# One list schedule for the whole program: the Strassen products of the first feed-forward product laid, four tiles at a time, between the matmuls of the second

## The chip, the core and the metric

The kernel runs on one core of a Trainium2 chip. The core has five engines with a queue of instructions each, worked off in order: TensorE (PE, matmuls into PSUM), VectorE (DVE), ScalarE (ACT), GpSimd (POOL) and SyncE (SP, which only issues transfers here). An engine waits on semaphores for the results of others. PSUM, where matmuls put their sums, has eight banks of 128 partitions by 512 fp32 values. The metric is the device time of one execution in microseconds (us), lower is better.

## The reference

Attention over keys and values pooled by eight, and then a feed-forward net with a PReLU. There are 8 batches of 576 tokens, 8 heads of 64, a model width of 512 and an inner width of 2048.

```python
k_p = k.reshape(B, H, Sp, pool, D).mean(axis=3)
v_p = v.reshape(B, H, Sp, pool, D).mean(axis=3)
scores = scale * np.matmul(q, k_p.transpose(0, 1, 3, 2))
scores = scores - np.max(scores, axis=-1, keepdims=True)
attn = np.exp(scores)
attn = attn / (np.sum(attn, axis=-1, keepdims=True) + 1e-09)
return np.matmul(attn, v_p).astype(np.float32)
...
x = np.ascontiguousarray(attn_out.transpose(0, 2, 1, 3)).reshape(B * S, H * D)
...
h = x @ w_in
g = np.maximum(h, 0.0) + alpha * np.minimum(h, 0.0)
return (g @ w_out).astype(np.float32)
```

## The kernel before

**Work and tiles.** The 4608 tokens are cut into nine chunks `c` of 512. Each fp32 operand is split into a high and a low fp16 part, and a product is three fp16 matmuls (low by high, high by low, high by high). `attention` makes a chunk's `x`; it is a chain over all engines with few and short PE instructions: maxima spread by a matmul (`pm`, L216), scores (`s`, L638), softmax, a transposing transfer to `aT`, and the mix with v (`x`, L648). The chain of chunk `c + 1` runs beside the feed-forward work of chunk `c`.

**The first feed-forward product** makes `h` in 16 tiles `f` of 128 inner columns. Chunks 0 and 1 take it plainly (`ffn1_products`, L814 to L816: 12 matmuls of 512 columns for a tile, 192 for a chunk). From chunk 2 on it is done after Strassen (`_Strassen`): four tiles are a block `b`, and a block is seven products of 12 matmuls of 256 columns (`product`, L936, psum tile `m`) where the plain way has eight; a chunk has 4 blocks, 28 products, 336 matmuls. DVE adds each finished product into two SBUF tiles `c` (`after`, L948, seven adds in a block; ACT copies the first one, L944), and `finish` scales (ACT, L960), applies the PReLU (DVE, L961) and splits into the fp16 pair `g` (ACT L962, POOL L963). The sums of the first weight that Strassen needs are made once, on POOL (`v`, L886), DVE (`u`, L889, four instructions, and `o`, L891) and ACT (L890), and kept in DRAM (`combine_w1`, eight steps `q`, during chunk 1); `weights` loads them back as `wt`, two for a block.

**The second product** (`ffn2`, L861 to L863) takes one of the chunk's four row tiles `i` at a time and runs over all 16 `f`: 48 matmuls of 512 columns into one bank, then ACT scales (`out_tile`, L851) and SP stores. It starts when the chunk's whole first product is through PE; so a chunk is one stretch of 336 short matmuls that DVE and POOL must follow, and one of 192 long ones that they need not.

**What sets the order.** Chunk 0, the weights' conversion and chunk 1's attention are laid by `start` with `_Plan`, a list scheduler in Python: each operation has an engine, an assumed duration, what it comes after, a rank and a buffer that it takes or gives; at each step the operation that can start first is issued, the lowest rank among near ones. `fill` puts idle matmuls (`idle`, L977) on PE where the plan sees a gap. From chunk 1 on the code is a plain loop, with the attention of the next chunk put in by counts (`behind`), and the compiler's own scheduler orders each engine's queue. PSUM is split into two tiles of two banks for attention and the conversion (`ps_s`) and four banks `ps_h`, which `m`, `h` and the output sums `o` share:

```python
ps_s = ctx.enter_context(tc.tile_pool(name="ps_s", bufs=2, space=PSUM))
ps_h = ctx.enter_context(tc.tile_pool(name="ps_h", bufs=4, space=PSUM))
...
            self.t[b, m] = ps = ps_h.tile([P, 2, HC], F32, tag="h", name="m")
            for p in range(2):
                for j in range(2):
                    w, x = self.lhs(2 * b + p, m, j), self.rhs(m, j)
                    for n, (lw, lx) in enumerate(((1, 0), (0, 1), (0, 0))):
                        nc.tensor.matmul(ps[:, p], w[:, lw], x[:, lx], start=(j == n == 0), stop=(j == 1 and n == 2))
...
    for b, m in [(b, m) for b in range(NB) for m in st.ORDER]:
        st.product(b, m)
        st.after(b, m)
        behind(-(-count // 25))
for i in range(TPC):
    ffn2(c, i)
    if i == 1:
        line.emit(mixes)
```

Of the kernel before, what the change touches and what calls it, by code (L numbers as in the profile page):

```python
# [13 lines left out]
ALU = mybir.AluOpType  # L14
# [46 lines left out]
def _new_b(c):  # L61
# [5 lines left out]
RK = dict(k_pool=2, ps1=5, ps2=8, s_pool=1, w2_dve=16, lo_dve=0, l1=226.38, step=42.02, l2=393.26, mx1=-998.39,  # L67
          mx1s=146.92, mx2=151.73, mx2s=21.09, grp=-5.46, grps=18.67, cv1=-108.04, cv1s=79.11, r2=-1083.65,
          cv2=835.35, cv2s=693.76, low1=871.6, low2=549.58, lo1=1355.61, lo2=54.48, sc=-185.32, pre=-1204.82,
          hi=-825.73, lo=214.7, step2=-280.35, a1=-96.45, al=2295.88, td=1395.43, ld1=71.07, ld2=2796.7,  # L70
          q0=-256.62, v0=75.31, sm0=125.88, sms0=20.85, mix0=-1030.58, q1=660.03, v1=140.65, sm1=189.37,
          sms1=-273.93, mix1=311.26)


ROOM = dict(d=3, W=8, L=4, f=4, e=3, v=3)
STEADY = dict(f=3, e=2, v=4)


class _Plan:
# [12 lines left out]
    def __init__(self, fill, **room):  # L92
        self.fill = fill
        self.ops, self.room, self.port = [], {k: n * [0.0] for k, n in room.items()}, 0.0

    def add(self, engine, us, emit, *after, rank=0.0, take=None, give=None, two=False):
        op = dict(engine=engine, us=us, emit=emit, after=after, rank=rank, n=len(self.ops),
                  take=take, give=(give,) if isinstance(give, str) else give or (), end=None,
                  two=two or engine == "Pool")
        self.ops.append(op)  # L100
        return op

    def start(self, op, free):
        if any(d["end"] is None for d in op["after"]) or (op["take"] and not self.room[op["take"]]):
            return None
        t = [free.get(op["engine"], 0.0)] + [d["end"] for d in op["after"]]
        if op["take"]:
            t.append(min(self.room[op["take"]]))
        if op["two"]:
            t.append(self.port)  # L110
        return max(t)

    def emit(self):
        free, left = {}, list(self.ops)
        while left:
            best = {}
            for op in left:
                t = self.start(op, free)
                if t is not None:
                    best.setdefault(op["engine"], []).append((t, op))  # L120
            picks = []
            for ready in best.values():
                t0 = min(t for t, _ in ready) + self.NEAR[ready[0][1]["engine"]]
                picks.append(min((x for x in ready if x[0] <= t0), key=lambda x: (x[1]["rank"], x[1]["n"])))
            t, op = min(picks, key=lambda x: (x[0], x[1]["n"]))
            if op["engine"] == "PE":
# [3 lines left out]
            free[op["engine"]] = t + op["us"]  # L130
            if op["two"]:
                self.port = t + op["us"]
            op["end"] = t + op["us"] + (self.DMA_HOP if op["engine"] == "SP" else self.HOP)
            if op["take"]:
                self.room[op["take"]].remove(min(self.room[op["take"]]))
            for kind in op["give"]:
                self.room[kind].append(op["end"])
            op["emit"]()
            left.remove(op)
# [3 lines left out]
def pooled_attention_prelu_ffn(ctx: ExitStack, tc: tile.TileContext, qT, kT, vT, kN, vN, w1, w2, alpha, out):  # L143
# [15 lines left out]
    gp = ctx.enter_context(tc.tile_pool(name="gp", bufs=NB))  # L159
    ps_s = ctx.enter_context(tc.tile_pool(name="ps_s", bufs=2, space=PSUM))  # L160
    ps_h = ctx.enter_context(tc.tile_pool(name="ps_h", bufs=4, space=PSUM))
    room = dict(ROOM)
    work = ExitStack()
    fp = work.enter_context(tc.tile_pool(name="fp", bufs=room["f"]))
# [700 lines left out]
    def ffn2(c, i):  # L865
        ps = ps_h.tile([P, DM], F32, tag="h", name="o")
        for f in range(NF):
            ffn2_step(c, i, f, ps)
# [253 lines left out]
```

## Time and profile before

| | us |
|---|---|
| median of 3 runs | 913.65 (913.49 to 917.79) |
| the profiled execution, its own time | 915.54 |
| its span, first to last instruction | 913.8 |
| PE busy | 824.7 |
| DVE busy | 608.3 |
| ACT busy | 459.6 |
| POOL busy | 410.2 |

The span is what the views of the trace divide up; the execution's own time is 1.74 us more. Busy time is a sum over the whole program and hides that DVE is nearly full in some stretches and nearly empty in others. A matmul's own duration is longer than the distance to the next one, since they are pipelined; what a stretch of matmuls costs is read from PE's busy time over the stretch, divided by their number. PEclk is the share of TensorE's full clock (2.4 GHz) that was granted; at 1.2 GHz it is a half.

### The profile page before, as it was taken

What the parts mean: (1) busy time and instruction counts of PE and PEld (TensorE: products, weight loads), DVE (VectorE), ACT (ScalarE), POOL (GpSimd) and SP (SyncE); (2) the same over time, 40 slices, a digit from 0 to 9 for tenths busy, and PEclk for the clock granted to TensorE, in tenths of its full rate; (3) what the DMA queues carried; (4) which work ended last, traced back from release to release, by engine and by line L of the source; (5) the groups of instructions that cost most, each with busy time, mean ns of one, the idle gap of its engine ahead of it and who ended that gap; (6) DMA issues with size and microseconds to landing.
All of it is one profiled execution on the core that took longest, in us unless ns stands there. A gap on an engine that the chain in (4) does not pass through costs nothing.

```text
span 913.8 us, 14931 instructions
## 1 busy us (share of the span) xinstructions
PE 824.7 (90%) x5953; PEld 503.4 (55%) x5953; DVE 608.3 (67%) x938; ACT 459.6 (50%) x760; POOL 410.2 (45%) x384
## 2 busy tenths in 40 slices
PE   6689988967998889979997999789978999899998
PEld 5454443423446744765475646654666468547843
DVE  5889997899537974597449844984499229733710
ACT  6879983635444464436335633563356336632420
POOL 1266577486505480357134823672247205800520
PEclk9979999988999899989999999999989999999999
DMA  9688323732644456427442754374437404902200
GB/s 340 228 239 340 98 65 81 244 123 88 151 141 144 146 150 172 148 89 226 128 154 103 208 128 155 125 218 117 154 129 207 115 24 163 249 28 82 104 14 33
DMA packets 106197, 133.68 MB, mean 146 GB/s; under 512 B 78320, under 2 KB 80944, under 8 KB 106128
## 3 DMA queue, kind: packets, MB, share of 16 engines
q1 hardware_dynamic: 106128, 132.74, 47.2%
q8 instruction: 46, 0.75, 0.3%
q14 instruction: 23, 0.19, 0.1%
HBM read 96.48 MB, written 16.78 MB: 124 GB/s over the span
## 4 chain that ended last, share of the span: by engine, by line
PE 51%; DVE 27%; ACT 7%; DMA 5%; issue 5%; POOL 5%; SPq 0%; DVEq 0%; ACTq 0%; POOLq 0%
PE o L861 12%; PE o L862 11%; PE o L863 11%; PE m L936 11%; DVE c L961 5%; DVE c L948 4%; DVE u L889 3%; POOL g L963 2%; DMA w<-w_dram 2%; DVE q L451 2%; PE x L648 2%; DMA ws<-o 2%; PE idle L977 2%; DVE t L824 1%; DVE o L891 1%
## 5 line engine op out<-in xcount | busy, mean ns | idle before, releaser
L936 PEld LDWEIGHTS <-wt 128*128 128x128 f16 x2352 | 230.5, 99 | 59.3 <-issue 26.9
L862 PE MATMUL o<-w,g 128*128 128x512 f16 x544 | 207.7, 382 | 2.9 <-POOL w L747 2.9
L963 POOL TENSOR_TENSOR g<-c,g 128x512 f16<-128x512 f32 x112 | 139.8, 1272 | 155.9 <-ACT g L962 151.7
L861 PE MATMUL o<-w,g 128*128 128x512 f16 x544 | 206.8, 383 | 1.0 <-DVE c L948 1.0
L863 PE MATMUL o<-w,g 128*128 128x512 f16 x544 | 206.6, 381 | 0.0
L948 DVE TENSOR_TENSOR c<-m,c 128x512 f32<-128x512 f32 x196 | 128.7, 680 | 93.7 <-PE m L936 91.7
L936 PE MATMUL m<-x,wt 128*128 128x256 f16 x1344 | 164.0, 278 | 13.5 <-DVE c L948 11.9
L472 POOL TENSOR_TENSOR vraw<-vraw 72x512 f32<-72x512 f32 (+1 forms) x56 | 59.9, 1090 | 179.6 <-DMA vraw<-vT_dram 145.9
L936 PE MATMUL m<-xt,wt 128*128 128x256 f16 x1008 | 123.4, 277 | 10.4 <-DVE c L948 10.4
L961 DVE SCALAR_TENSOR_TENSOR c<-c,al 128x512 f32<-128x512 f32 x112 | 108.0, 992 | 4.8 <-ACT c L960 4.8
L851 ACT ACTIVATE o<-o,os 128x512 f32<-128x512 f32 x34 | 23.3, 687 | 163.9 <-PE o L863 163.9
L960 ACT ACTIVATE c<-c,rp 128x512 f32<-128x512 f32 x112 | 73.3, 712 | 49.4 <-DVE c L948 49.3
L863 PEld LDWEIGHTS <-g 128*128 128x128 f16 x576 | 56.8, 99 | 72.3 <-issue 5.4
L861 PEld LDWEIGHTS <-g 128*128 128x128 f16 x576 | 56.9, 99 | 70.6 <-issue 3.9
L862 PEld LDWEIGHTS <-g 128*128 128x128 f16 x576 | 56.8, 99 | 66.9 <-issue 2.1
L962 ACT CAST g<-c 128x512 f16<-128x512 f32 x112 | 65.1, 615 | 30.4 <-DVE c L961 29.8
L601 DVE TENSOR_TENSOR xf<-xf 128x256 f32<-128x256 f32 x56 | 23.8, 424 | 84.4 <-ACT xf L596 82.9
L814 PE MATMUL h<-x,w 128*128 128x512 f16 x128 | 51.7, 404 | 11.2 <-ACT t L820 9.9
L546 ACT CAST apad<-e 128x576 f16<-128x576 f32 x72 | 44.7, 668 | 32.5 <-POOL e L541 27.8
L541 POOL TENSOR_TENSOR e<-e,sm 128x576 f32<-128x576 f32 x35 | 44.8, 1281 | 31.9 <-DVE sm L539 10.6
L835 POOL TENSOR_TENSOR g<-t,g 128x512 f16<-128x512 f32 x32 | 42.3, 1330 | 29.0 <-ACT g L832 28.9
L815 PE MATMUL h<-x,w 128*128 128x512 f16 x128 | 51.9, 405 | 2.9 <-DVE x L580 2.9
(152 smaller groups left out, 1092.9 us busy)
## 6 DMA issues: line engine op xcount, KB each, us to landing
wt<-ws SPq DMA_DIRECT2D x56, 896.0 KB
w<-w_dram SPq DMA_DIRECT2D x16, 1024.0 KB
out_dram<-o SPq DMA_DIRECT2D x36, 256.0 KB
qraw<-qT_dram SPq DMA_DIRECT2D x17, 512.0 KB
vraw<-vT_dram SPq DMA_DIRECT2D x28, 288.0 KB
kraw<-kT_dram SPq DMA_DIRECT2D x12, 576.0 KB
ws<-o SPq DMA_DIRECT2D x8, 512.0 KB
ws<-w SPq DMA_DIRECT2D x8, 256.0 KB
```

The lines of the kernel that those rows point to most:

```text
L472: nc.gpsimd.tensor_tensor(out=o, in0=y, in1=z, op=ALU.add)
L814: nc.tensor.matmul(ps, w[:, 1, ks_], x[:, 0], start=(n == 0), stop=False)
L815: nc.tensor.matmul(ps, w[:, 0, ks_], x[:, 1], start=False, stop=False)
L861: nc.tensor.matmul(ps, g[:, 1, ts_], w[:, 0], start=(f == 0), stop=False)
L862: nc.tensor.matmul(ps, g[:, 0, ts_], w[:, 1], start=False, stop=False)
L863: nc.tensor.matmul(ps, g[:, 0, ts_], w[:, 0], start=False, stop=(f == NF - 1))
L936: nc.tensor.matmul(ps[:, p], w[:, lw], x[:, lx], start=(j == n == 0), stop=(j == 1 and n == 2))
L948: nc.vector.tensor_tensor(out=self.part(b, *o), in0=ps, in1=self.part(b, *i), op=ALU.add)
L960: nc.scalar.activation(u, u, AF.Copy, scale=rp[:, f:f + 1])
L961: nc.vector.scalar_tensor_tensor(out=u, in0=u, scalar=al[:, f:f + 1], in1=u, op0=ALU.mult, op1=ALU.max)
L962: nc.scalar.copy(out=g[:, 0, p], in_=u)
L963: nc.gpsimd.tensor_tensor(out=g[:, 1, p], in0=u, in1=g[:, 0, p], op=ALU.subtract)
```

## The change

1. `start` no longer issues its plan: the rest of the program is added to the same `_Plan`, and one list schedule orders all five engines from the first instruction to the last. The numbers in `RK` and the room for buffers are new; the first stage's plan has new ranks.
2. `steady` lays PE's order for chunks 1 to 8: the items of a block of the first product (seven Strassen products, or four plain tiles) and eight pieces of the second product of the block before, in turn. A piece is one row tile `i` with two of the block's four `f`, six matmuls; the four row tiles are summed over the chunk in the four banks of `ps_h`, and scaled and stored when block 3 is in. The last block of a chunk lies between the products of the next chunk's first.
3. After the first stage PSUM is split anew: one tile of two banks for attention (`ps_s2`), two banks for the first product (`ps_m`), four for the output sums.
4. The seven products come in another order, with the adds that go with it (seven as before), and the fp16 pairs `g` of two blocks are held in place of four.
5. `combine_w1` is ordered by the plan, behind the last matmul of chunk 0's second product. Attention's operations are planned with a margin behind what they wait for, and added time on DVE and ACT.

PE's instructions are the same in kind and number, but for the idle ones: 248 where there were 179.

```diff
-RK = dict(k_pool=2, ps1=5, ps2=8, s_pool=1, w2_dve=16, lo_dve=0, l1=226.38, step=42.02, l2=393.26, mx1=-998.39,
+RK = dict(k_pool=1, ps1=7, ps2=8, s_pool=1, w2_dve=16, lo_dve=0, l1=620.91, step=116.52, l2=1225.44, mx1=-690.6,
...
-ROOM = dict(d=3, W=8, L=4, f=4, e=3, v=3)
+ROOM = dict(d=3, W=8, L=4, f=3, e=3, v=3, qp=2, vp=2, aT=1, S=2, h=4, m=0, g=0, x=0, X=0)
+THEN = dict(S=1, m=2, g=2, x=1, X=1)
+MORE = {"DVE": 0.25, "ACT": 0.1}
+AHEAD = {"PE": 2.0, "DVE": 0.3, "ACT": 0.3, "Pool": 0.3, "SP": 0.3}
...
-        ORDER = "1675234"
+        ORDER = "1652374"
...
+    def switch():
+        nonlocal ps_s, ps_m, gp, xp2
+        work.close()
+        ps_s = work.enter_context(tc.tile_pool(name="ps_s2", bufs=THEN["S"], space=PSUM))
+        ps_m = work.enter_context(tc.tile_pool(name="ps_m", bufs=THEN["m"], space=PSUM))
+        gp = work.enter_context(tc.tile_pool(name="gp2", bufs=THEN["g"]))
...
+        def pe(us, emit, *after, **kw):
+            last_pe[:] = [plan.add("PE", us, emit, *after, *last_pe, rank=FFN, ahead=-_Plan.HOP, **kw)]
+            return last_pe[0]
+
+        def att(engine, us, emit, *after, **kw):
+            return plan.add(engine, us + MORE.get(engine, 0.0), emit, *after, ahead=AHEAD[engine], **kw)
+
+        def finish(c, f, scale, prelu, hi, lo, at, rank, take=None, give=(), free=None):
+            x = plan.add("ACT", 0.71, scale, *at, rank=rank, take=take, give=free)
+            x = plan.add("DVE", 0.99, prelu, x, rank=rank)
+            x = plan.add("ACT", 0.62, hi, x, rank=rank, take=None if (c, f // 4) in g_at else "g")
+            g_at.setdefault((c, f // 4), {})[f] = plan.add("Pool", 1.27, lo, x, rank=rank, give=give)
...
+        def out_items(c, b):
+            for k in range(2):
+                for i in range(TPC):
+                    def item(k=k, i=i):
+                        first, final = b == k == 0, b == NB - 1 and k == 1
+                        fs = (4 * b + k, 4 * b + 2 + k)
+
+                        def products():
+                            if first:
+                                acc[c, i] = ps_h.tile([P, DM], F32, tag="h", name="o")
+                            for f in fs:
+                                ffn2_step(c, i, f, acc[c, i], first and f == fs[0], final and f == fs[1])
+                        x = pe(1.3, products, *(g_at[c, b][f] for f in fs), take="h" if first else None,
+                               give="g" if k == 1 and i == TPC - 1 else None)
...
+            k = 0
+            for j, item in enumerate(one):
+                item()
+                while two and k < (j + 1) * len(two) // len(one):
+                    two[k]()
+                    k += 1
```

The order on PE in the middle of a chunk. Here is PE's queue at the end of a chunk's 336 short matmuls before (`m` is a Strassen product, `o` an output sum, `wt`, `x` and `xt` the operands of the first product, `g` and `w` those of the second):

```order
4965 L936 MATMUL m<-xt,wt 128x256
4966 L936 LDWEIGHTS wt
4967 L936 MATMUL m<-xt,wt 128x256
4968 L936 LDWEIGHTS wt
4969 L936 MATMUL m<-xt,wt 128x256
4970 L861 LDWEIGHTS g
4971 L861 MATMUL o<-w_755,g 128x512
4972 L862 LDWEIGHTS g
4973 L862 MATMUL o<-w_755,g 128x512
```

And one of the places in the changed queue where a piece of the second product ends and the next product begins:

```order
4139 L883 MATMUL o<-w_855,g 128x512
4140 L881 LDWEIGHTS g
4141 L881 MATMUL o<-w_855,g 128x512
4142 L882 LDWEIGHTS g
4143 L882 MATMUL o<-w_855,g 128x512
4144 L883 LDWEIGHTS g
4145 L883 MATMUL o<-w_855,g 128x512
4146 L959 LDWEIGHTS wt
4147 L959 MATMUL m<-xt,wt 128x256
4148 L959 LDWEIGHTS wt
4149 L959 MATMUL m<-xt,wt 128x256
```

Before, such a border stands once in a chunk, with 336 matmuls ahead of it and 192 (and the mix) behind; now 12 `m` and 6 `o` (twice in a block 12) take turns throughout.

The order on DVE where the sums of the first weight are made. Before, they stand between the PReLUs of chunk 1 (`t`) and the pooling of chunk 2's keys (`ks`):

```order
216 L889 TENSOR_TENSOR u<-v,u 128x256
217 L891 TENSOR_TENSOR o_1978<-u,o_1978 128x1024
218 L824 SCALAR_TENSOR_TENSOR t<-t,al 128x512
219 L889 TENSOR_TENSOR u<-v 128x256 x2
220 L889 TENSOR_TENSOR u<-u,v 128x256
221 L384 TENSOR_REDUCE ks<-kraw 128x144
222 L889 TENSOR_TENSOR u<-v,u 128x256
```

Now the last two of the eight stand at the end of chunk 1's work, the seventh ahead of the split (`x`, `xt`) that makes chunk 2's second half of `x` ready, the eighth between it and the first add of a Strassen product (`c<-m,c`):

```order
300 L620 TENSOR_TENSOR xf<-xf 128x256 x4
301 L914 TENSOR_TENSOR o_2726<-u,o_2726 128x1024
302 L627 TENSOR_TENSOR x_2731<-xf,x_2731 128x1024
303 L628 TENSOR_TENSOR xt<-xf,xt 128x768
304 L910 TENSOR_TENSOR u<-v 128x256
305 L910 TENSOR_TENSOR u<-u,v 128x256
306 L910 TENSOR_TENSOR u<-v 128x256
307 L910 TENSOR_TENSOR u<-v,u 128x256
308 L465 SCALAR_TENSOR_TENSOR q_2350<-qraw,s,q_2350 128x1024
309 L914 TENSOR_TENSOR o_2767<-u,o_2767 128x1024
310 L465 SCALAR_TENSOR_TENSOR q_2388<-qraw,s,q_2388 128x1024
311 L972 TENSOR_TENSOR c<-m,c 128x2x256
```

Two of the eight lay in the first stage before, ahead of chunk 1's PReLUs; now none does. And on PE, where chunk 0's first product (`h`) is through, the scores of chunk 1 followed at once before, and now 68 idle matmuls stand ahead of them:

```order
1006 L230 LDWEIGHTS ones
1007 L230 MATMUL pm<-pd,ones 128x128
1008 L230 LDWEIGHTS ones
1009 L230 MATMUL pm<-pd,ones 128x128
1010 L994 LDWEIGHTS pool
1011 L994 MATMUL idle<-pool 128x256
1012 L994 LDWEIGHTS pool
1013 L994 MATMUL idle<-pool 128x256
```

## Rows read from the trace of the kernel before

**Rows 1.** Busy time by stretch: length, each engine (instructions), PEclk, DMA share, GB/s.

```profile
61.30:112.60 51.30, 46.53 (x271) 20.82 (x270) 47.64 (x63) 45.06 (x68) 29.82 (x25) 0.93 0.67 246
112.60:166.60 54.00, 47.02 (x277) 21.34 (x274) 47.00 (x70) 33.59 (x72) 36.90 (x36) 0.97 0.31 74
166.60:230.00 63.40, 49.63 (x269) 21.84 (x269) 56.85 (x67) 32.24 (x53) 42.42 (x32) 0.88 0.45 156
230.00:276.00 46.00, 45.27 (x250) 20.76 (x249) 18.74 (x32) 19.34 (x29) 12.91 (x14) 0.98 0.57 145
558.50:605.00 46.50, 38.84 (x425) 33.38 (x424) 42.13 (x66) 25.22 (x42) 29.86 (x28) 1.00 0.54 163
605.00:650.00 45.00, 44.80 (x237) 21.34 (x237) 19.43 (x32) 18.71 (x29) 13.60 (x13) 1.00 0.51 144
831.90:868.50 36.60, 36.60 (x338) 32.81 (x336) 25.97 (x39) 17.37 (x30) 13.63 (x12) 1.00 0.30 109
868.50:913.80 45.30, 41.52 (x193) 18.63 (x191) 3.34 (x5) 7.02 (x12) 4.93 (x4) 1.00 0.06 24
```

**Rows 2.** PE's waits from 276 to 832 us: total, times, longest.

```profile
PE m L936 <- DVE c L948: 22.3, 15, 4.0
PE pm L216 <- ACT pd L213: 17.4, 4, 5.2
```

**Rows 3.** Time line of PE and of the last ACT instruction: start, length, what [idle before].

```profile
45.41 14.05 PE L977 MATMUL idle<-pool 128*128 128x256 f16 x103
296.01 2.21 PE L936 MATMUL m<-x,wt 128*128 128x256 f16 x12 [4.05 <-DVE c L948]
299.43 2.72 PE L936 MATMUL m<-xt,wt 128*128 128x256 f16 x12 [1.22 <-DVE c L948]
301.94 2.19 PE L936 MATMUL m<-x,wt 128*128 128x256 f16 x12
410.85 1.47 PE L936 MATMUL m<-x,wt 128*128 128x256 f16 x12 [0.64 <-DVE c L948]
910.11 0.69 ACT L851 ACTIVATE o<-o,os 128x512 f32<-128x512 f32 x1 [9.72 <-PE o L863]
```

**Rows 4.** PE's waits from 60 to 166 us, the first stage, two of the longest.

```profile
PE o L862 <- POOL w L747: 2.9, 1, 2.9
PE s L638 <- ACT e L526: 2.7, 1, 2.7
```

**Rows 5.** Groups of DVE instructions, by shape: busy us, mean ns, idle before.

```profile
L948 DVE TENSOR_TENSOR c<-m,c 128x512 f32<-128x512 f32 x196 | 128.7, 680 | 93.7 <-PE m L936 91.7 <-PE pm L216 0.6 <-issue 0.5
L961 DVE SCALAR_TENSOR_TENSOR c<-c,al 128x512 f32<-128x512 f32 x112 | 108.0, 992 | 4.8 <-ACT c L960 4.8
L889 DVE TENSOR_TENSOR u<-v 128x256 f32<-128x256 f32 x16 | 17.3, 1118 | 3.8 <-DMA ws<-o 3.7
L891 DVE TENSOR_TENSOR o<-u,o 128x1024 f16<-128x1024 f32 x8 | 13.9, 1732 | 5.5 <-ACT o L890 5.5
L889 DVE TENSOR_TENSOR u<-u,v 128x256 f32<-128x256 f32 x8 | 7.0, 879 | 0.0
L889 DVE TENSOR_TENSOR u<-v,u 128x256 f32<-128x256 f32 x8 | 6.1, 761 | 0.2
```

**Rows 6.** Time line of DVE: the PReLU with POOL at work, and with POOL idle.

```profile
417.30 3.12 DVE L961 SCALAR_TENSOR_TENSOR c<-c,al 128x512 f32<-128x512 f32 x2
841.72 2.73 DVE L961 SCALAR_TENSOR_TENSOR c<-c,al 128x512 f32<-128x512 f32 x4
166.15 0.75 DVE L889 TENSOR_TENSOR u<-v 128x256 f32<-128x256 f32 x2
163.22 1.21 DVE L891 TENSOR_TENSOR o<-u,o 128x1024 f16<-128x1024 f32 x1
```

**Rows 7.** The page, two groups: busy us, mean ns, idle before.

```profile
L963 POOL TENSOR_TENSOR g<-c,g 128x512 f16<-128x512 f32 x112 | 139.8, 1272 | 155.9 <-ACT g L962 151.7
L960 ACT ACTIVATE c<-c,rp 128x512 f32<-128x512 f32 x112 | 73.3, 712 | 49.4 <-DVE c L948 49.3
```

More of the change, by code (lines that the diff above doesn't have):

```diff
@@ L100, in add @@
         self.ops.append(op)
         return op
[L103 to L111, printed above, removed]
-    def emit(self):
[L114 to L120, printed above, removed]
-            picks = []
[L122 to L126, printed above, removed]
+    def emit(self):
+        ops, free = self.ops, {}
+        mine = {id(op) for op in ops}
+        follow, left, since, ready = [[] for _ in ops], [], len(ops) * [0.0], {}
+        for op in ops:
+            after = [d for d in op["after"] if id(d) in mine]
+            for d in after:
+                follow[d["n"]].append(op)
+            left.append(len(after))
+            if not after:
+                ready.setdefault(op["engine"], {})[op["n"]] = op
+        for _ in ops:
+            picks = []
+            for engine, some in ready.items():
+                at = []
+                for n, op in some.items():
+                    t = max(free.get(engine, 0.0), since[n], self.port if op["two"] else 0.0)
+                    need = {k: op["take"].count(k) for k in op["take"]}
+                    if any(len(self.room[k]) < x for k, x in need.items()):
+                        continue
+                    t = max([t] + [sorted(self.room[k])[x - 1] for k, x in need.items()])
+                    at.append((t, op["rank"], n))
+                if at:
+                    t0 = min(at)[0] + self.NEAR[engine]
+                    picks.append(min((x for x in at if x[0] <= t0), key=lambda x: x[1:]))
+            t, _, n = min(picks, key=lambda x: (x[0], x[2]))
+            op = ops[n]
+            engine = op["engine"]
+            if engine == "PE" and self.fill:
@@ L966, in pooled_attention_prelu_ffn, with join, row, g_tile @@
+        def join(self, b, m, n):
+            o, i = self.JOIN[m][n]
+            nc.vector.tensor_tensor(out=self.part(b, o), in0=self.t[b, m], in1=self.part(b, i), op=ALU.add)
+        def row(self, b, i, p):
+            return self.t[b, i][:, p].rearrange("p k t -> p (k t)"), 4 * b + 2 * p + i
+    def g_tile(c, f):
+        if (c, f // 4) not in gs:
+            gs[c, f // 4] = gp.tile([P, 2, 4, CH], F16, tag="g", name="g")
+        return gs[c, f // 4][:, :, f % 4]
     GROUPS = ((0, 2), (2, 6), (6, 10), (10, NF))
-    def start():
+    def start(plan):
@@ L1089, in pooled_attention_prelu_ffn @@
+    plan = _Plan(**ROOM)
+    steady(plan, *start(plan))
+    with tc.manual_schedule(engines={ENG.SP, ENG.PE, ENG.DVE, ENG.Activation, ENG.Pool}):
+        plan.emit()
     work.close()
```

335 lines of the change are left out of this document (181 added, 154 removed).

## The prediction

> **What bounds the kernel now.** I read the page first, then busy time by stretch, then PE's waits, then the time line where a wait had to be priced. PE is busy for 824.7 us of 913.8, 90%, but that says nothing of where the other 10% lies. The stretches do [rows 1]. Take one chunk: from 558.5 to 605 us its Strassen products run, and PE has 38.84 us of work in 46.5 while DVE is busy for 42.13 (91%). From 605 to 650 its second product runs, PE is full, and DVE has 19.43 us to do in 45. So the two engines swap the part of the bound twice in a chunk. The whole chunk takes 91.5 us for 83.6 us of PE work (38.84 + 44.80, at full clock): 7.9 us are lost, all but a little in the first half. I take it as the pattern of the six chunks that have a next chunk's attention beside their products.
>
> PE's waits from the first product to the last chunk name the causes [rows 2]: 22.3 us waiting for DVE's adds to free a product's bank, and 17.4 us in four waits of a `pm` for ACT, which are attention's small matmuls standing in PE's queue with all the products behind them. The last chunk has no attention beside it: 336 products in 36.6 us without a gap (0.109 us each), then 192 matmuls in 41.5 (0.216 each) [rows 1]. That is what PE can do.
>
> Chunk 1, from 166.6 to 276, is worse: 109.4 us, in which PE is busy for 94.9 at a clock below full, DVE for 75.6 and POOL for 55.3 [rows 1].
>
> **First stage, to 166.6 us.** The work is the same, but the ranks are new. Two things move in it. The 68 idle matmuls ahead of chunk 1's scores cost 7.4 us at 0.109 each, or 9.3 at the 0.136 of the group of 103 [rows 3]; they stand where the plan expects a gap. Against that, the second product loses 5.6 us there already in two waits [rows 4], and two of the eight weight sums leave the stage, each 5.5 us of DVE (17.3 + 13.9 + 7.0 + 6.1 = 44.3 for eight [rows 5]), which is busy 87% in its second half [rows 1]. I take the end as unchanged, 166.6, with 160 and 172 as bounds: both waits gone and the fill hidden in the gap, or the fill on top of a part of them.
>
> **Chunk 1, up to the first Strassen product.** On PE this is the plain first product, 192 x 0.216 = 41.5 us, three quarters of the second (31), and some 5 us of attention (83.6 less 36.6 and 41.5): 77.5. DVE decides it. The order shows that seven of the eight sums, the 16 PReLUs and chunk 2's attention lie ahead of the split that makes chunk 2's `x` ready. Before, chunk 1 held six sums and took 75.6 us of DVE; with one sum more it is 81, and if the pooling of chunk 2's keys, drawn into the first stage, takes some 3 us off, 78. At 100% of DVE that is 78 us; at the 93% and 87% that the plan reached in the two halves of the first stage [rows 1] it is 84 and 90. I take 87, and 78 and 94 as bounds. So the first product comes at 166.6 + 87 = 253.6, where it came at 276; but a quarter of chunk 1's second product is then still to do.
>
> A rule of the Trainium skill bears on this. First the rows: two PReLUs took 3.12 us with POOL at work, four took 2.73 with POOL idle, 0.68 each [rows 6]. The skill's page "SBUF — State Buffer", section "Who interferes with whom", says that a DVE instruction with two SBUF inputs and a GpSimd instruction that reads SBUF shut each other out for a whole instruction. By that the stretch cannot be shorter than POOL's 55.3 us plus DVE's two-operand work at its undisturbed price: 16 x 0.68 for the PReLUs and seven sums at 2.7 (0.75 for two of the four `u`, 1.21 for `o` [rows 6]), 85 us, and the splits of q, k, v and x would come on top. By this the total would be 859 at the least, and my lower bound of 78 for the stretch would fall away.
>
> **The rest.** PE's work from there is a quarter of chunk 1's second product (10.4 us), six chunks at 83.6, and the last at 36.6 + 41.5: 590.1 us. What hides the other engines' work is the even mix. A product now comes every 2.8 us (1.31 for itself, 8 pieces of 1.3 among 7 products) and brings 61.6 us / 28 = 2.2 us of DVE work with it (42.13 + 19.43 for the chunk [rows 1]). DVE goes from 91% in the products' half to 74% throughout. A bank is asked for again two products later; an add takes 0.68 us [rows 5], so it may come some 3 us late before PE notices. The `g` of a block's first tiles must be ready one product into the next block, about 9 us after the product that completes them. Their path is an add 0.68, two scalings at 0.71, a PReLU 0.99 [rows 5, 7], a cast like a scaling and POOL's 1.27 [rows 7], 5 us and the hand-overs, say 6. If DVE or POOL is held up there by more than 3 us, PE stands. Attention's PE steps are now planned 2 us behind what they wait for; each that is later still holds everything behind it.
>
> What waits remain I cannot read from a row. From below it is nothing, from above the 7.9 us of today's chunk. As DVE's free share rises from 9% to 26%, I take a quarter of that, 2 us for a chunk, 14 for seven. Transfers are the same in number and now spread: a block's two `wt` have a whole block, 19.6 us, to land.
>
> **The end.** The last block's second product stands alone, 10.4 us, already counted. After the last matmul the last row tile is scaled and stored: 913.8 - 910.1 = 3.7 us [rows 3].
>
> **Sum:** 166.6 + 87 + 590.1 + 14 + 3.7 = 861.4 of span. The profiled execution's own time is 1.7 above its span, and the median of the runs 1.9 below that execution's time, so the span stands for the median: I predict 861 us, 5.8% faster. For this kernel 0.5%, 4.6 us, is about what a measurement can tell from no change.
>
> **Rivals.**
> *Cleaner than that.* No waits remain and DVE is full in chunk 1: 160 + 78 + 590.1 + 3.7 = 832; halfway to it, 847. For it: PE ran 336 products without a gap when no attention was beside them [rows 1]. Against: the first stage is laid by the same planner and kept waits. Chance 0.15.
>
> *The waits only spread.* Queues are fixed by assumed times; a DVE instruction that POOL holds up (3.12 for 1.37 us) makes the next add late wherever it stands. Then a chunk keeps its 7.9 us: 861.4 - 14 + 55 = 902. For it: in the planned first stage PE waits 5.6 us in the 54 of its second half [rows 4], the same tenth as in a chunk. Against: DVE is 87% busy there, not 74%. Chance 0.15.
>
> *The change doesn't do what it says:* `x` of the next chunk is never ready in time, and PE stands at the border where it used to run the second product. To come out level it would stand (913.8 - 861.4) / 6 = 8.7 us at each of six borders. Against: attention has the whole chunk for itself as before, and DVE, ACT and POOL all have room in it. Chance 0.03.
>
> *Slower: one attention tile in PSUM.* With one `ps_s2` instead of two, each of the nine PE steps of a chunk's attention (four scores, three `pm`, two mixes) must wait until DVE or ACT has left the tile, and the products wait behind it. Such a wait costs 4.35 us today (17.4 / 4 [rows 2]). If all nine waited it would be 39 us for a chunk, and 1,080 us in all. It decides from (913.8 - 847.4) / 54 = 1.2 us for each step on. Against: 84 us hold nine turns of a few us each. Chance 0.03.
>
> *Slower: the clock.* Rows first: after a wait of 4.05 us, 36 products took 7.1 us, where 12 take 1.47 and 36 about 3.9; after a wait of 0.64 the next 12 took 1.47 [rows 3]. The change gives the products two banks where they had four, so that short waits may come in every block. If the clock fell once in each of 28 blocks at 3.2 us, the time would be 861 + 90 = 951; it decides from 16 falls on. The trace is against it, since the short wait cost no clock. Chance 0.02. The Trainium skill ("TensorE: Matmul & The Clock Gate", section "A second HAM failure mode: psum-queue depth-cycling") tells of a kernel in which going round PSUM banks made short idle times between groups of matmuls, and these alone made the clock swing; by that rule this rival would be likelier than I make it.
>
> **How the numbers follow.** The forecast's own range, 848 to 880, holds 0.62. It and the first two rivals end faster: 0.92. The third is the no-change case, 0.03, and the last two make 0.05 slower. For 8 in 10, I cut the cleaner case below 842 and the spread one above 888.
>
> **What would show it.** Right: from the first product on, stretches of 84 to 87 us for a chunk, PE above 95% busy and DVE near 74% in any slice, no slice with PE full and DVE under half; PEclk at 1.00; PE's waits for `c` and `pm` together under 15 us; the first product near 254. The first stage is wrong if chunk 1's first plain matmul comes outside 160 to 172, chunk 1 if DVE is below 85% in it and PE still waits. The forecast fails if chunks take 90 us or more: then PE's longest waits tell whether it is banks, `g` or attention.

## The result and the profile after

The changed kernel takes 875.01 us (median of 4 runs, 874.30 to 880.52), the kernel before 913.57 beside it: the ratio is 0.958, with a 95% interval of 0.953 to 0.963. It is 4.2% faster. The forecast was 861, its range 842 to 888; the profiled execution spans 873.4 us and took 875.13.

The first view is the page of the changed kernel, busy tenths in 40 slices of 21.8 us.

```profile
PE   6889999889959998999998999799999999999998
DVE  5889997697897679759775878777786574343432
PEclk9999999999979999999999999899999999999999
```

PE is at nine tenths or more in nearly all slices from the second quarter on, and up to some 720 us the slices of DVE no longer swing between full and under half, as the two halves of a chunk did before [rows 1]. Two dents stand out: the twelfth slice (240 to 262 us), where PE's clock falls too, and the 26th (546 to 568).

The same execution by stretch (length, each engine's busy time, PEclk, DMA share, GB/s): chunk 1 up to the first Strassen product, what follows it, then three stretches from the later chunks.

```profile
163.00:254.00 91.00, 81.55 (x472) 36.78 (x473) 77.95 (x103) 49.85 (x75) 57.48 (x47) 0.95 0.59 169
254.00:276.00 22.00, 17.78 (x174) 11.55 (x174) 18.82 (x27) 4.88 (x7) 7.40 (x7) 0.83 0.26 92
276.00:360.00 84.00, 79.74 (x676) 52.09 (x674) 66.09 (x105) 46.89 (x75) 43.93 (x47) 1.00 0.64 174
600.00:682.00 82.00, 82.00 (x653) 53.63 (x652) 60.42 (x102) 42.29 (x65) 32.80 (x31) 1.00 0.45 130
764.00:846.00 82.00, 82.00 (x559) 54.56 (x558) 33.57 (x47) 24.71 (x41) 20.17 (x17) 1.00 0.23 82
```

In the stretch from 600 to 682 us PE has no gap at all, and DVE is busy for 60.42 of 82, 74%. From 276 to 360 us it is 79%, and from 764 to 846, where no attention stands beside the products, 41%. Chunk 1 and what follows it is another matter: 91 us with 81.55 of PE work, then 22 us with 17.78.

PE's waits from 254 us to its end (total, times, longest) stand against [rows 2]:

```profile
PE o L881 <- ACT o L871: 6.4, 1, 6.4
PE m L959 <- DVE x L627: 5.9, 2, 4.2
PE m L959 <- ACT x L623: 4.9, 1, 4.9
PE pm L230 <- ACT pd L227: 2.4, 1, 2.4
PE m L959 <- ACT c L968: 1.8, 2, 0.9
PE o L881 <- POOL g L1118: 1.7, 2, 1.3
PE s L660 <- DVE e L547: 1.5, 1, 1.5
PE x L670 <- ACT xf L615: 1.1, 1, 1.1
PE m L959 <- DVE c L972: 1.0, 2, 0.5
```

The 22.3 us for DVE's adds have become 1.0, and the 17.4 us of small attention matmuls 2.4. What is left is of another kind, and it sits in a few places. PE's time line (start, length, what, [idle before]) shows them:

```profile
162.97 0.61 PE L836 MATMUL h<-x,w 128*128 128x512 f16 x1 [3.02 <-DVE pt L233]
253.99 0.37 PE L959 MATMUL m<-x,wt 128*128 128x256 f16 x1 [4.85 <-ACT x L623]
258.58 1.87 PE L959 MATMUL m<-x,wt 128*128 128x256 f16 x8 [4.22 <-DVE x L627]
551.72 0.59 PE L881 MATMUL o<-w,g 128*128 128x512 f16 x1 [6.44 <-ACT o L871]
```

The second and third belong to the first Strassen products, which wait for the second half of chunk 2's `x` (three matmuls of the first ran at 248.65, ahead of the wait). The fourth is a border between chunks: the second product of the next chunk needs an accumulator that ACT has not yet copied out. Why `x` was late is read from DVE's time line ahead of it:

```profile
247.71 0.42 DVE L910 TENSOR_TENSOR u<-v 128x256 f32<-128x256 f32 x1
248.16 0.42 DVE L910 TENSOR_TENSOR u<-u,v 128x256 f32<-128x256 f32 x1
248.50 0.42 DVE L910 TENSOR_TENSOR u<-v 128x256 f32<-128x256 f32 x1
248.84 1.37 DVE L910 TENSOR_TENSOR u<-v,u 128x256 f32<-128x256 f32 x1
250.14 3.98 DVE L620 TENSOR_TENSOR xf<-xf 128x256 f32<-128x256 f32 x4
254.04 2.28 DVE L914 TENSOR_TENSOR o<-u,o 128x1024 f16<-128x1024 f32 x1
256.25 2.28 DVE L627 TENSOR_TENSOR x<-xf,x 128x1024 f16<-128x1024 f32 x1
```

A weight sum (`u`, `o`) stands around the four sums `xf`, and the last `u`, the `xf`, the `o` and the `x` all take two to three times what they take elsewhere (`u` 0.42, `o` and `x` 1.22, the four `xf` 1.79 in a run below). POOL was at work beside them almost without a break, from 248.61 us on.

### The profile page after: what moved, and what is told of

Read it like the earlier page. It is cut to its first block, busy times and chain, and to the rows that moved or that the text cites. A ratio compares the mean times of both kernels' runs of the same rounds, so it can differ in the third digit from the quotient of the medians.

```text
span 873.4 us, 15051 instructions
## 1 busy us (share of the span) xinstructions
PE 818.3 (94%) x6022; PEld 503.3 (58%) x6022; DVE 620.1 (71%) x939; ACT 461.6 (53%) x760; POOL 395.2 (45%) x381
## 4 chain that ended last, share of the span: by engine, by line
PE 81%; DVE 9%; ACT 4%; DMA 4%; issue 1%; SPq 0%; POOL 0%; ACTq 0%
PE m L959 27%; PE o L881 12%; PE o L882 12%; PE o L883 12%; PE h L837 3%; PE h L838 3%; PE h L836 3%; PE x L670 2%; PE s L660 2%; DVE c L1111 2%; PE idle L994 1%; DMA out_dram<-o 1%; DMA qraw<-qT_dram 1%; ACT e L543 1%; DMA nat<-kN_dram 1%
## 5 line engine op out<-in xcount | busy, mean ns | idle before, releaser
L1118 POOL TENSOR_TENSOR g<-c,g 128x512 f16<-128x512 f32 x112 | 134.7, 1213 | 288.1 <-ACT g L1115 190.9
L972 DVE TENSOR_TENSOR c<-m,c 128x512 f32<-128x512 f32 x196 | 134.6, 687 | 142.1 <-PE m L959 133.4
L959 PE MATMUL m<-x,wt 128*128 128x256 f16 x1344 | 166.6, 274 | 13.5 <-DVE x L627 5.9
L1107 ACT ACTIVATE c<-c,rp 128x512 f32<-128x512 f32 x112 | 75.4, 714 | 112.0 <-DVE c L972 111.6
L1115 ACT CAST g<-c 128x512 f16<-128x512 f32 x112 | 68.2, 617 | 50.3 <-DVE c L1111 49.8
L558 POOL TENSOR_TENSOR e<-e,sm 128x576 f32<-128x576 f32 x35 | 42.7, 1220 | 43.0 <-DVE sm L556 35.3
L836 PE MATMUL h<-x,w 128*128 128x512 f16 x128 | 49.9, 390 | 6.8 <-ACT t L842 3.6
L566 POOL TENSOR_TENSOR apad<-e,apad 128x448 f16<-128x448 f32 x36 | 39.8, 1106 | 27.2 <-ACT apad L563 22.6
L837 PE MATMUL h<-x,w 128*128 128x512 f16 x128 | 49.8, 389 | 1.9 <-DVE x L598 1.9
L838 PE MATMUL h<-x,w 128*128 128x512 f16 x128 | 49.8, 389 | 0.0
```

The source lines that it names most:

```text
L836: nc.tensor.matmul(ps, w[:, 1, ks_], x[:, 0], start=(n == 0), stop=False)
L837: nc.tensor.matmul(ps, w[:, 0, ks_], x[:, 1], start=False, stop=False)
L838: nc.tensor.matmul(ps, w[:, 0, ks_], x[:, 0], start=False, stop=(n == NK - 1))
L972: nc.vector.tensor_tensor(out=self.part(b, o), in0=self.t[b, m], in1=self.part(b, i), op=ALU.add)
L1107: nc.scalar.activation(u, u, AF.Copy, scale=rp[:, f:f + 1])
L1115: nc.scalar.copy(out=g_tile(c, f)[:, 0], in_=st.row(b, i, p)[0])
```

## The experiments

Twelve kernels were run, each an edit of the changed kernel. What the prediction leaned on most, the mix of products and pieces, came first. The experiments were measured on several chips, on which the kernel before had medians of 912.4 to 915.3 us; so a difference of a few us between two of them is no more certain than their ratios to the kernel before, which are given with a 95% interval.

**Blocks apart.**

```diff
-            for j, item in enumerate(one):
-                item()
-                while two and k < (j + 1) * len(two) // len(one):
...
-            for item in two[k:]:
+            for item in one + two:
                 item()
```

> The same list schedule, buffers and margins, but in each block all seven Strassen products (9.2 us) stand ahead of all eight pieces of the second product (10.4 us) of the block before; nothing else is edited. Theory (the gain is the even mix, product by piece): an add is asked for every 1.3 us again for 9 us at a stretch, with two banks behind it, so PE's waits for DVE's adds come back, at least 0.7 us in each of 24 blocks, 17 us or more in all (1.0 us in the changed kernel), and the time is 890 to 905. Rival (blocks of four f tiles would do, whatever the order inside): waits for the adds under 5 us and 872 to 879.

Measured: 873.71 us (872.40 to 876.00), ratio 0.957 (0.955 to 0.960), the same as the changed kernel. The theory fell, the rival held for the time. PE's waits from 254 us on:

```profile
PE m L959 <- DVE c L972: 6.9, 9, 2.6
PE m L959 <- ACT c L968: 4.4, 2, 2.8
```

The waits for banks did grow, from 2.8 us (1.0 and 1.8) to 11.3, but they came 11 times in 28 blocks (24 in the expectation was a miscount, as are 168 products for 196 further down), not in each. The equal time is in part luck: the 8.5 us more at the banks were mostly made up by the 6.44 us at the border, which were gone, and whether the order took them away or chance did was not separated. (In the changed kernel two pieces stand together once in a block, not twice as the account of the change has it.) Seven products in a row mostly run free: PE has two banks of lead, and DVE's seven adds of 0.69 us fit into 9.2 us when its other work can wait.

**Pairs of blocks apart.**

```diff
-            if n:
-                two = list(out_items(1 + (n - 1) // NB, (n - 1) % NB))
...
+            for item in one:
                 item()
...
+            if c < NC and b % 2 == 1:
+                for b_ in range(b - 1, b + 1):
+                    for item in out_items(c, b_):
+                        item()
```

> The products of two blocks (18.4 us) stand together, then the pieces of the second product of the same two blocks (20.8 us); no alternation, and no lag of a block between a block's products and its second product beyond that. Still one list schedule, two banks, two g blocks. Theory: half of before's separation is back, so DVE swaps between over 90% and under half again; 905 to 930, with waits for the adds of more than 25 us. Rival (the gain came from the first stage, the early start of the weight sums and the margins of attention): under 885.

Measured: 893.97 us (893.68 to 894.33), ratio 0.979 (0.978 to 0.981). The theory's sign held, its size was too large: half of the gain is gone.

```profile
PE m L959 <- DVE c L972: 22.8, 22, 2.5
PE h L836 <- ACT t L842: 12.2, 5, 5.5
```

Over the whole span the waits for DVE's adds are back at the 22.3 us of [rows 2], and in chunk 1 plain products wait 12.2 us for their scalings (3.6 in the changed kernel). The edit also takes away the lag of a block between a block's products and its second product; no wait for `g` shows for that. So with two banks the grain matters between one block and two, and a finer one brought nothing that can be measured.

**One bank, and one bank with blocks apart.** The two runs ask what the alternation is still good for.

```diff
-THEN = dict(S=1, m=2, g=2, x=1, X=1)
+THEN = dict(S=1, m=1, g=2, x=1, X=1)
```

> One bank for the Strassen products in place of two, products and pieces alternating as in the changed kernel. In the run with blocks apart and two banks the order inside a block made no difference. Theory (the two banks hide the adds, the alternation is a second cover for the same thing): with one bank each product waits only where a piece of 1.3 us does not cover an add of 0.69 and its hand-overs, 0.2 to 0.5 us for each of 168 products, and the time is 905 to 960. Rival (DVE is often more than 1.3 us late, so that both covers are needed): over 980.

> One bank, and the seven products of a block ahead of the eight pieces. Theory (without the second bank only the alternation could cover the adds): 6 of 7 products in a block wait for an add or copy and two hand-overs, some 1.0 to 1.4 us, 144 times: 1,015 to 1,080. Rival (the order inside a block is of no account whatever the banks): within 10 us of the run with one bank and alternation.

Measured, in one run each: 911.51 and 1066.84 us. Both lie in the range of the theory. With alternation, though, the waits are 28 of 1.1 us on average, not a little at every product. The waits over the span, first with alternation, then with blocks apart:

```profile
PE m L959 <- DVE c L972: 30.3, 28, 1.9
```

```profile
PE m L959 <- DVE c L972: 143.6, 137, 2.9
PE m L959 <- ACT c L968: 21.8, 27, 5.1
```

With one bank the alternation is worth 155 us, with two it is worth nothing that can be measured. The second bank hides the adds in either order; the alternation alone hides most of them, and 36.5 us of time are left (911.5 against 875.0). The second run also says something of the clock; it is told at the end.

**No weight sums.** The edit empties the four compute steps of `combine_w1` and stores the unsummed weights.

```diff
-            nc.gpsimd.tensor_tensor(out=v(), in0=src()[:, :, 0], in1=src()[:, :, 1], op=ALU.add)
+            pass
...
-                nc.vector.tensor_tensor(out=u()[:, i], in0=a, in1=b, op=op)
+            pass
```

> Leaves out the arithmetic of the eight weight sums (the sum on POOL, the four sums on DVE, the cast on ACT and the subtraction on DVE); the transfer that stored their result stores the unsummed fp16 weights in its place, so Strassen's products get wrong weights of the same size. The order of everything else on every engine is as in the changed kernel. Theory (chunk 1 is set by DVE and POOL, which the sums fill): chunk 2's x is ready ahead of PE, the two waits of 4.85 and 4.22 us ahead of the first products fall under 1 us together, the first product comes 78 to 83 us after chunk 0's second product ends where it took 94, and the time is 858 to 865. Rival (the chain of chunk 2's attention, its hand-overs and its single xf tile set it, whatever DVE has to do): the first product within 3 us of where it was and 871 to 876.

Measured: 867.74 us (864.14 to 868.09), ratio 0.951 (0.949 to 0.952), about 7 us less; between the theory's range and the rival's. The stretch from chunk 1's first plain matmul to the first product:

```profile
159.00:243.50 84.50, 80.44 (x469) 36.36 (x470) 41.47 (x67) 42.11 (x67) 34.66 (x37) 0.96 0.70 194
```

The first matmuls of the product come at its end, and behind a wait for `x` of 0.98 us it goes on at 244.94, 86.0 us after chunk 1's first plain matmul at 158.91, where the changed kernel took 91.0 (162.97 to 253.99). The next wait for `x` is 2.00 us in place of 4.22. DVE is now busy for half of the stretch, so PE's own work (80.44) sets it. The sums reach into the first stage too. In the changed kernel a DVE instruction of one column stands ahead of what chunk 1's first plain matmul waits for, beside POOL's first weight sum (160.31 to 162.42 us):

```profile
159.75 2.69 DVE L865 TENSOR_TENSOR os<-wsc,ev 128x1 f32<-128x1 f32 x1
```

Without the sums it took 0.42 us, and that matmul waited 0.75 us in place of 3.02. All the sums together, about half of DVE's work in chunk 1, are worth some 7 us by the medians (the two profiled executions lie 11.0 us apart).

**Two sums behind x.**

```diff
-w_at[q] = combine_w1(att, q, ATT + SUMS["at"] + SUMS["step"] * q + SUMS["later"] * (q > 3), *sums)
+w_at[q] = combine_w1(att, q, ATT + SUMS["at"] + SUMS["step"] * q + SUMS["later"] * (q > 3), *sums, *(xr[2] if q > 5 else []))
```

> One dependence added in the plan: the weight sums of the last two f pairs wait for both halves of chunk 2's x, so that the u and o of the seventh sum no longer stand between the two halves in DVE's queue. Theory (the sums in front of x cost the wait): the second half of x is ready about 5 us earlier, PE's waits for x fall from 9.1 us to under 4, and the time is 867 to 871. Rival (the single xf tile and the queue positions bind): 873 to 877, waits for x still 7 us or more.

Measured: 870.24 us (865.42 to 874.41), ratio 0.953 (0.949 to 0.957), an interval that overlaps that of the changed kernel; the median lies in the theory's range. The waits for `x` are gone, as the theory had it, but another of nearly the same size took their place. DVE's time line:

```profile
238.92 1.79 DVE L620 TENSOR_TENSOR xf<-xf 128x256 f32<-128x256 f32 x4
249.00 6.73 DVE L620 TENSOR_TENSOR xf<-xf 128x256 f32<-128x256 f32 x4
```

POOL's beside the second of these, and what PE did behind it:

```profile
250.06 2.20 POOL L486 TENSOR_TENSOR vraw<-vraw 72x256 f32<-72x256 f32 x2
252.22 0.41 POOL L486 TENSOR_TENSOR vs<-vraw 72x128 f32<-72x128 f32 x1
252.59 2.10 POOL L904 TENSOR_TENSOR v<-w 128x1024 f32<-128x1024 f16 x1
```

```profile
257.37 1.43 PE L660 MATMUL s<-kt,q 64*64 64x72 f16 x48 [7.96 <-DVE e L547]
```

The same four sums took 1.79 us with POOL idle and 6.73 with POOL busy. Scores of chunk 3 stood in PE's queue behind that, for the one attention tile in PSUM, and all products behind the scores.

**No margins.** The plan's two dictionaries `AHEAD` and `MORE` were emptied, together and each alone.

```diff
-MORE = {"DVE": 0.25, "ACT": 0.1}
-AHEAD = {"PE": 2.0, "DVE": 0.3, "ACT": 0.3, "Pool": 0.3, "SP": 0.3}
+MORE = {}
+AHEAD = {"PE": 0.0, "DVE": 0.0, "ACT": 0.0, "Pool": 0.0, "SP": 0.0}
```

> The margins with which the plan lays attention from chunk 2 on (2.0 us for a PE step behind what it waits for, 0.3 for the other engines, 0.25 and 0.1 us more for a step of DVE and ACT) are set to nothing; all else as in the changed kernel. Theory (the margins are what took attention's PE steps out of PE's way: four waits for pm cost 17.4 us in the kernel before and three cost 4.8 in the changed one): PE's waits in front of s, pm and the mixes' x rise from 5 us after 300 us of the span to 20 or more, and the time is 888 to 900. Rival (the attention of a whole chunk spread over 84 us is early enough anyhow): 868 to 879.

Measured: 858.62 us (856.71 to 859.92), ratio 0.936 (0.932 to 0.941). The theory fell, and the time lies below the rival's range too: the margins cost 16.4 us by the medians, and some 20 by the ratios. PE's waits from 300 us on, of which the changed kernel has 17.5:

```profile
PE m L959 <- DVE c L972: 3.4, 2, 2.6
PE pm L230 <- ACT pd L227: 2.4, 3, 1.4
PE pm L230 <- DVE pt L233: 0.7, 1, 0.7
```

They are 7.4 us in all, and not one is longer than 2.6. And ahead of chunk 2's products there is one wait for `x` of 3.8 us, in place of 4.85 and 4.22.

> Only the delays of attention's steps behind what they wait for are set to nothing (2.0 us for PE's, 0.3 for the others'); the 0.25 and 0.1 us that the plan adds to DVE's and ACT's steps of attention stay. Without either the time was 858.6. Theory (the delays make chunk 2's x late and put attention's PE steps where PE does not need them): most of the 16 us come from here, 858 to 865. Rival (the padded durations make the plan think DVE fuller than it is, and lay its work too late): 868 to 876.

> The other half of the margins alone: the padding of DVE's and ACT's steps of attention (0.25 and 0.1 us in the plan) is taken away, the delays (2.0 and 0.3 us) stay. So far: both, 875.0; without the delays, 870.9; without either, 858.6. Theory (the two costs add, and the padding costs the greater part because it makes the plan lay attention's steps behind later products than they could be done with): 861 to 866. Rival (only without both does chunk 2's attention come early enough; either alone delays it): 869 to 876.

Measured: without the delays 870.86 us (868.68 to 872.79), ratio 0.954 (0.951 to 0.957); without the padding 867.50 (865.79 to 869.63), ratio 0.950 (0.947 to 0.952). For the delays alone the rival held, and the interval overlaps that of the changed kernel; for the padding alone the time fell between theory and rival. By the medians it is some 4 and 7.5 us, and 16.4 for both: the sum, with 5 us on top. The 4 are not clear of noise, and so the size of what comes on top isn't either. In both runs a wait shows that was not in the sum, here with the delays left out, then with the padding left out:

```profile
255.42 1.43 PE L660 MATMUL s<-kt,q 64*64 64x72 f16 x48 [8.89 <-ACT xf L615]
```

```profile
255.96 0.91 PE L660 MATMUL s<-kt,q 64*128 64x72 f16 x24 [11.08 <-ACT xf L615]
```

It is chunk 3's first scores again, waiting for the one tile, which holds chunk 2's second mix until ACT can scale it into `xf`. That needs the one `xf` buffer, which is held until DVE has split the first half. The place in PE's queue, ahead of the products, comes from the plan.

**The idle matmuls.**

```diff
-            if acc or n <= 0:
+            if acc or n <= 0 or gs:
```

> The 68 idle matmuls ahead of chunk 1's scores are left out; the 180 at the start stay. Theory (they stand in a gap that ends with DVE's split of q at 112.97 us and hold back nothing): PE waits there for 7 to 8 us instead, chunk 1's scores still start at 113, and the time is within 3 us of 875. First rival (they cost what they take): 867 to 869. Second rival (they keep PE's clock up for the second product): the granted clock after 113 us is below 0.9 for several us where it is 1.00 now, and the time is 877 to 882.

Measured: 877.58 us (876.15 to 879.32), ratio 0.958 (0.954 to 0.962), no difference to the changed kernel that can be told. The first rival fell; the time lies in the ranges of the theory and of the second rival, so it does not decide between them. The scores and the stretches behind them:

```profile
113.16 2.26 PE L660 MATMUL s<-kt,q 64*128 64x72 f16 x72 [7.42 <-DVE q L465]
```

```profile
113.00:125.00 12.00, 11.84 (x132) 6.16 (x132) 9.58 (x19) 10.14 (x36) 7.60 (x10) 0.78 0.19 51
125.00:158.00 33.00, 33.00 (x187) 14.94 (x185) 25.00 (x35) 19.96 (x34) 22.93 (x23) 1.00 0.76 173
```

The 68 matmuls stood in a real gap, as the theory had it. The second rival saw a true thing, the clock at 0.78 for 12 us where it was 1.00; the last matmuls of the stage came 2.1 us later (a `pm` at 161.68 instead of 159.61). That need not be the clock's doing, since in the two runs with one bank, whose edits leave this stage alone, the same `pm` came at 159.27 and 161.37. Chunk 1's first plain matmul then waited 1.59 us for that `pm`'s maximum instead of 3.02, and started 0.6 us later than in the changed kernel.

**POOL away from x, and all three.** No margins, and the next chunk's attention begins behind the whole `x` of the chunk before.

```diff
-xr[c + 1], td = attention(att, c + 1, _new_b(c + 1), ATT + 100.0 * c, behind=[*td[:1], loaded])
+xr[c + 1], td = attention(att, c + 1, _new_b(c + 1), ATT + 100.0 * c, behind=[*(xr[c] if c > 1 else td[:1]), loaded])
```

> No margins, and one dependence changed: the loads of the next chunk's attention (from chunk 3 on) wait for the whole x of the chunk before instead of its first transposition. So POOL has no values to halve while DVE makes x. Theory (DVE's sums for x are slow because POOL works in SBUF beside them: the second half's four took 3.98 us in the changed kernel and 6.73 with the sums put behind x, where four undisturbed ones took 1.79): they take 2.5 us or less, PE's waits for x ahead of the first products fall from 3.8 us to under 1, and the time is 852 to 857. Rival (attention of one chunk at a time comes too late for the chunks that follow): new waits of over 5 us at the borders of chunks 3 to 6, 862 or more.

> No margins, the loads of the next attention behind x, and the last two weight sums behind both halves of chunk 2's x. Theory: each takes something away from in front of x, and chunk 2's products start without a wait: 848 to 855, the lowest of all. Rival (the two sums then stand among the adds of chunk 2's first blocks, and their blocks' weights come late): 857 or more, with waits for adds or for the weights in chunk 2.

Measured: 847.78 us (846.63 to 853.59), ratio 0.931 (0.927 to 0.935), the fastest of all and lower than the theory said; and 851.98 (850.11 to 852.99), ratio 0.934 (0.931 to 0.936), which is within the theory's range but not the lowest: with the intervals overlapping, the two sums behind `x` bring nothing more. Against the run without margins alone the first gains 11 us by the medians but only some 5 by the ratios (0.931 against 0.936), and these intervals overlap too: that it gains is likely, not shown. The first, in the time line of DVE and of PE:

```profile
241.68 1.79 DVE L620 TENSOR_TENSOR xf<-xf 128x256 f32<-128x256 f32 x4
```

```profile
244.86 0.60 PE L959 MATMUL m<-x,wt 128*128 128x256 f16 x4
246.58 1.03 PE L959 MATMUL m<-x,wt 128*128 128x256 f16 x8 [1.11 <-DVE x L627]
```

The second half's sums take the undisturbed 1.79 us (3.68 without margins alone), and PE waits 1.11 us where it waited 9.07 in the changed kernel and 3.8 without margins alone. That is some 3 us of the gain. From 158 us on PE's waits are 7 us fewer in all, and the granted clock over the span is 0.992 in place of 0.986; the edit also keeps chunk 3's scores out of PE's queue ahead of chunk 2's products, and which of the two did more was not separated.

## Why the prediction was right, and where it was off

The span is 873.4 us, the sum was 861.4. Term by term:

**First stage.** The term was 166.6 with bounds 160 and 172; chunk 1's first plain matmul starts at 162.97. It is 3.6 us better. The two waits of [rows 4] are gone, and the idle matmuls cost nothing that can be measured, as the run without them shows. What is new is the wait of 3.02 us at the stage's end, 2.3 of it beside POOL's first weight sum.

**Chunk 1 up to the first Strassen product.** The term was 87; it took 91.0 (162.97 to 253.99), 4.0 more, inside the bounds of 78 and 94. The two misses cancel, which is luck: the product comes at 253.99, where 253.6 was forecast. DVE is busy for 77.95 of 91, 86%. "DVE decides it" was only partly right. When the sums were taken out and DVE stood at half, the stretch was 86.0 us long, most of it PE's own work, which I had at 77.5 and which was 80.44 there, at a clock of 0.96. What the sums hold up is thus the 5.0 us between 86.0 and 91.0, and 2.2 of the wait that follows, both through the second half of `x`, and the 2.3 us ahead of the stretch.

The Trainium skill, "SBUF — State Buffer", section "Who interferes with whom", has it that a DVE instruction with two SBUF inputs contends with a GpSimd instruction that reads SBUF; the estimate made from it, that this stretch could not be under 85 us, was not undercut. That is no proof of the rule. It is borne out by the four sums of `xf`, at 1.79 us with POOL idle and 6.73 with POOL busy, by their return to 1.79 when POOL's work was moved away, and by the one-column instruction that took 2.69 us beside POOL's sum and 0.42 without it.

**PE's work and the end.** From 253.99 to the last matmul's end at 869.6 are 615.6 us, where the sum had 590.1 of work and 14 of waits. The tail is 3.8 against 3.7.

**The remaining waits are the term that was mis-sized:** 25.5 us, not 14; they are 21.9 of waits and 3.6 of PE work beyond the 590.1. I had spread them, "2 us for a chunk", by DVE's free share. That share came out as forecast, 74%, from 600 to 682 us, and the banks cost 1.0 us for DVE's adds. But the loss is not spread. From 600 to 682 and from 764 to 846 us PE has none. 4.2 us are the second wait for chunk 2's `x`, 6.4 one chunk border, and some 11 ten shorter waits. The 3.6 us go with work at the lower clock behind three of these waits (around 260, 473 and 552 us the second product's matmuls come one every 0.43 us, 0.22 elsewhere). Single waits of a fixed order were the cost, not a share of DVE's load in every chunk.

**The signs.** The waits for `c` and `pm` together stayed small (5.2 us). The even chunks did not come: from one chunk's first Strassen weight load to the next chunk's it is 98.4 us (a quarter of chunk 1's second product is in it), 86.4, 90.0, 92.3, 85.2 and 79.9, where 84 to 87 was the sign of being right. And DVE stood at 41% beside a full PE from 764 to 846 us, where the prediction wanted 74% in any slice.

**Where the gain lies.** The spans differ by 40.4 us. From the first Strassen product to the last matmul's end it was 634.2 us before (275.9 to 910.1), in which PE was busy for 591.2; now it is 615.6, with 593.7 of PE work, and 10.4 of that is chunk 1's last quarter. So some 29 us were won there, an estimate from these numbers: 21 of waits (43.0 before, 21.9 now) and 8 of work at a fuller clock (591.2 where 579.7 would do at full clock, 593.7 where 590.1 would). The prediction counted PE's work at full clock throughout and had no term of its own for the second part.

**A cost left out.** The margins entered the prediction only as cover ("planned 2 us behind what they wait for"), at no price. They cost 16.4 us, more than the whole miss. Without them the time is 858.6, and PE's waits from 158 us on fall from 34.3 to 20.4 us. How a margin makes a wait I read so: the plan puts a step that it thinks late behind other work in the same queue, and on the chip that work then does delay it. This was argued, not followed step by step.

**Right for a reason that was too strong.** "What hides the other engines' work is the even mix. A product now comes every 2.8 us." Laying the second product between the Strassen products did move DVE's work under PE's, but whole blocks in turn do it as well (873.7 against 875.0). Two blocks at a time lose half the gain, and the chunk at a time of the kernel before loses all. A chunk's products apart, in the new schedule, were not run; so how much of the gain the other edits share at that grain stays open.

**The rivals.** Waits that only spread (902) did not come. The one attention tile, which had to cost 1.2 us at each of 54 steps to decide, showed itself at single steps only: 8.0, 8.9 and 11.1 us in three of the experiments, 7.6 and 6.0 with one bank, 5.8 with pairs of blocks apart. The clock fell in the changed kernel only behind waits for other things than a bank. (The 336 and 36 products of the prediction are matmuls, 28 and 3 products.) The cleaner case, halfway at 847, is about what the best experiment reached (847.8), by edits that this change does not contain.

The median lies 1.6 us above the span, where I had let the one stand for the other: that is the rest of the 14 us.

## What to carry to other kernels

When two engines take turns at being the bound, find the grain at which their work has to alternate before writing a fine one: here the block, because two banks of lead cover what happens inside it. In a fixed order, price the safety margins of the plan too, and look for the single buffer whose late release holds an engine's whole queue. And when an instruction's time doubles, look at what POOL is doing beside it, not only at its own chain.

## What the hardware showed beside that

Short waits for a bank brought the clock down in one part of a run and not in another. With one bank and blocks apart PE had 31 waits, 29.4 us in all, from 560 to 700 us (25.7 in 25 times for DVE, 3.7 in 6 for ACT), and the granted clock of that stretch was 1.00, the higher of the two levels:

```profile
560.00:700.00 140.00, 110.56 (x839) 69.43 (x838) 64.56 (x103) 50.02 (x77) 36.46 (x32) 1.00 0.31 97
```

From 840 us on PE's waits in the same run are of the same kind, none longer than 2.05 us. Yet four times, the first at 847 us, the clock fell to the lower level behind such waits, and the second product's matmuls came one every 0.43 us:

```profile
835.00:870.00 35.00, 26.56 (x170) 16.85 (x169) 9.72 (x15) 8.48 (x13) 4.98 (x4) 0.95 0.23 84
846.79 2.11 PE L959 MATMUL m<-xt,wt 128*128 128x256 f16 x12 [2.05 <-DVE c L972]
848.69 0.63 PE L881 MATMUL o<-w,g 128*128 128x512 f16 x1
```

The Trainium skill, "TensorE: Matmul & The Clock Gate", section "A second HAM failure mode: psum-queue depth-cycling", tells of a kernel in which going round PSUM banks made the clock swing; the trace agrees from 840 us on and does not from 560 to 700, where the waits are of 0.95 us on average. Nor did the length of a single wait decide it. Behind one of 3.02 us chunk 1's first plain matmuls of the changed kernel ran at the lower level (one every 0.43 us), and behind one of 1.59 us in the run without the idle matmuls at the higher (one every 0.22). But in the run with POOL away from `x` they ran at the higher level behind a longer wait:

```profile
162.60 0.39 PE L836 MATMUL h<-x,w 128*128 128x512 f16 x1 [3.43 <-DVE pt L233]
```

What else decides it, these runs do not show.
